# Where the low parts of the first MLP's weights and activations are subtracted, and how the decay products are formed

## The chip, the cores and the metric

The kernel runs on one core of one Trainium2 chip. The metric is the device time of one execution in microseconds. The core has five engines that each run their own queue in order: TensorE (PE in the profile; PEld is its weight load), VectorE (DVE), ScalarE (ACT), GpSimd (POOL), and SyncE (SP), which issues transfers. GpSimd issues transfers too.

## What is computed

Three parts follow each other: a linear attention with a decay per step, an MLP over all tokens, and a second stage with eight experts of which each token uses two.

```python
for t in range(S):                                   # 4 batches, 8 heads, S = 768, D = 48
    S_re, S_im = a[t] * (S_re + i S_im) + outer(k[t], v[t])     # a[t] complex, |a| <= 0.999
    y[t] = q[t] @ S_re
x = y.reshape(3072, 384)
h = x @ w_in                                         # 384 x 2048, w_in and w_out are float64
g = where(h > 0, h, exp(h) - 1)
x = g @ w_out                                        # 2048 x 384
logits = x @ w_gate + log1p(exp(x @ w_noise)) * noise
out[tok] = sum over the top two e of weight * relu(x @ w1[e]) @ w2[e]
```

## The kernel before

**Numbers.** TensorE runs its large products in the fast 32-bit format (fp32r), which keeps fewer bits than float32. Each factor is therefore split into a high part (the value rounded to fp32r) and a low part (the value less the high part), and a product is three products: high by high, high by low, low by high.

**Stages.** The attention is cut into 12 units (6 chunks of 128 steps by 2 pairs of batches). A unit has pieces `p` (magnitude and angle of the decay), `o`, `t` (sine, cosine, arctangent on ScalarE), `m` (decay products), `a`, `b` (scores, state, output `y`, its transpose `xt` with high and low part). The first MLP of unit u (`f`) follows in eight steps `s`: `l1(s)` makes 2 x 128 rows of `h` on TensorE (18 products, line 850), ScalarE and VectorE make `ge` out of it (lines 854 to 856), ScalarE its high part `gh` (line 859), VectorE its low part `gl` (line 860), and `l2(s)`, issued two steps later (`LAG = 2`), multiplies with the second weights (line 874). After every second unit, `route` picks the experts and eight indirect writes on GpSimd's queue (line 967) put the tokens into `table`. The eight experts follow.

**The first MLP's weights.** They come as float64 in 32 blocks of 128 x 384 (16 of `w_in`, 16 of `w_out`). For each block GpSimd issues the transfer (line 483), VectorE decodes the 64-bit values into `wf` with four instructions (lines 467 to 469 and 484), ScalarE rounds them to the high part (lines 507, 525), and TensorE forms the low part in PSUM: `ident` times `raw` in float32, then `minus` (the negative identity) times the high part is added to it (lines 509 and 510; 521 and 527 for `w_out`). ScalarE copies it out (lines 511, 528). For `w_out` the gate's weights are multiplied in as well: three transposes (line 517), a copy (519), three narrow products (523), a copy of the high part (526). The tiles of this stage use the same buffers as the MLP's: `raw` those of `xh` and `xl`, `wf` those of `gh` and `gl`, `woT` that of `ge`, `wtp` that of `ph`, `wlo` that of `y2`. So the MLP of unit 0 starts only behind the last block.

**The decay products.** `m_pieces` makes the running product over 128 steps with VectorE multiplications: seven over strides of 8 (`cm1`), four that double the reach (`cm2`) and one wide one (`cm3`), lines 633, 639 and 644, for each of the 12 units.

**Order.** `PAR` gives each piece a place in program order. Then `arrange` takes all instructions, gives each a cost by engine and shape, and lays them out by a list schedule (longest remaining path first); that order is each engine's queue. A tile of a ring of buffers may not start before the first users of the one before it (`roots`). `PAR['EARLY']` is 8, and there are 8 pairs of blocks, so that the branches `late` of `fetch`, `load_w_in` and `load_w_out` are never taken and place `x` is empty.

Of the kernel before, what the change touches and what calls it, by code (L numbers as in the profile page):

```python
# [27 lines left out]
def arrange(tc):  # L28
# [58 lines left out]
    def cost(n):  # L87
        i, k, c = ins[n], kinds[n], cells[n]
        if eng[n] == "PE":
# [25 lines left out]
        if eng[n] == "DVE":  # L115
# [16 lines left out]
        if k == "Memset":  # L132
            return 100 + c * .55, 100 + c * .55
        return 25, 25
# [5 lines left out]
    for n, i in enumerate(ins):  # L140
        e = eng[n]
        p = prev.get(e)
        if e == "PE" and p is not None and kinds[n] == kinds[p] == "Matmult":
            a, b = acc[p][0], acc[n][0]
            same = a[0] == b[0]
# [205 lines left out]
def tile_kernel(ctx, tc, q, k, v, a_re, a_im, w_in, w_out, w_gate, w_noise, noise, w1, w2, qp, kp, vp, ap,  # L351
# [42 lines left out]
    minus = consts.tile([128, 128], F32R, name="minus")  # L394
    ts(minus, jp, 0.0, -1.0, op0=OP.is_equal, op1=OP.mult)
# [62 lines left out]
    wbad = consts.tile([128, 2, 2 * FB], F32, name="wbad")  # L458
# [12 lines left out]
    def fetch(piece, f, n, late):  # L471

        tagf = "ge" if late else ("gh", "gl")[n % 2]
        t = wf.tile([128, Dm], F32, name="wf", tag=tagf, bufs=2)
        if not wide:
            nc.gpsimd.dma_start(*piece(f, 0, Dm, t))
            return t
        for z, (a, b) in enumerate(((0, 256), (256, Dm)) if late else ((0, Dm),)):
            if late:
                raw = wa.tile([128, 256, 2], I32, name="raw", tag="n4", bufs=4)[:, :b - a]  # L480
            else:
                raw = wf.tile([128, Dm, 2], I32, name="raw", tag=("xh", "xl")[n % 2], bufs=2)
            nc.gpsimd.dma_start(*piece(f, a, b, raw))
            nc.vector.tensor_reduce(wbad[:, z, n:n + 1], raw[:, :, 1].bitcast(F32), axis=AX.X, op=OP.min,
                                    apply_absolute_value=True)
            decode(raw, t[:, a:b])
        return t
# [15 lines left out]
    def load_w_in(f, late):  # L503
        raw = fetch(w_in_piece, f, f, late)
        WI[f] = [wts.tile([128, KD, 128], F32R, name=f"wi{x}", tag="wi") for x in "hl"]
# [7 lines left out]
    def load_w_out(f, late):  # L513
        raw = fetch(w_out_piece, f, FB + f, late)
# [9 lines left out]
        hi, lo = WO[f] = [wts.tile([128, WC], F32R, name=f"wo{x}", tag="wo") for x in "hl"]  # L524
# [1054 lines left out]
```

## Time and profile before

| | us |
|---|---|
| median of 3 executions | 1257.93 (1257.11 to 1259.96) |
| profiled execution, its own time | 1253.42 |
| span of that execution, first to last instruction | 1251.6 |
| busy in the span: TensorE | 1160.8 (93%) |
| VectorE | 786.7 (63%) |
| ScalarE | 648.9 (52%) |
| GpSimd | 234.4 (19%) |

The span is what the trace shows; 1.82 us of the execution lie outside of it. Busy shares over the whole span mix stages with different limits, so the rows below are by stretch: the weights are loaded from 0 to 131.5 us (beside the attention of the first units), attention and first MLP run from there to about 642 us, the last units' MLP to about 800 us, and the experts to the end.

### The profile page before, as it was taken

To read this page: it belongs to the slowest core of one execution; us is meant where nothing else is said; L and a number is where in the kernel's file an instruction comes from. 1 tells how busy PE (TensorE), PEld (TensorE's weight loads), DVE (VectorE), ACT (ScalarE), POOL (GpSimd) and SP (SyncE) were. 2 spreads that over 40 slices of the span, in tenths; PEclk is the share of its full clock that TensorE was granted. 3 is DMA by queue.
4 is the path that set the end of the run, shared out by engine and by line. 5 is a ranking of instruction groups with operands and counts; after the bars stand their busy time and mean duration, and the time that the engine had idled before them with its cause. 6 is when DMAs were issued, how large, how long until landed. Compare 5 with 4: busy or idle time off the path is not lost.

```text
span 1251.6 us, 22832 instructions
## 1 busy us (share of the span) xinstructions
PE 1160.8 (93%) x8821; PEld 1070.9 (86%) x8821; DVE 786.7 (63%) x1782; ACT 648.9 (52%) x1299; POOL 234.4 (19%) x265
## 2 busy tenths in 40 slices
PE   4786998999999999899999999799999999999997
PEld 2464988888998999899999898789898989898996
DVE  5798998987987979697863556344434343443322
ACT  6877876768776777576554464332323232332111
POOL 2111000002002000200200302432424242424222
PEclk9697999999999999899999999999999999999999
DMA  6345520220220202120100133343424242423111
GB/s 218 118 160 179 182 81 24 72 94 12 84 75 21 81 22 79 18 92 31 30 11 28 52 103 119 109 127 96 134 90 136 83 137 85 131 85 108 36 45 34
DMA packets 64309, 107.05 MB, mean 86 GB/s; under 512 B 19967, under 2 KB 46310, under 8 KB 64192
## 3 DMA queue, kind: packets, MB, share of 16 engines
q1 hardware_dynamic: 50096, 65.65, 16.9%
q0 software_dynamic: 14096, 39.86, 10.2%
q8 instruction: 71, 1.16, 0.4%
q14 instruction: 46, 0.38, 0.1%
HBM read 86.98 MB, written 20.70 MB: 86 GB/s over the span
## 4 chain that ended last, share of the span: by engine, by line
PE 51%; DVE 25%; issue 14%; ACT 6%; DMA 2%; POOL 2%; POOLq 0%; SPq 0%; DVEq 0%; ACTq 0%
PE mpo L1096 18%; PE mph L1074 17%; PE ph L850 4%; PE y L874 4%; DVE gl L860 2%; DVE ge L856 2%; DVE E L633 2%; DVE X L701 2%; PE mtp L1059 1%; DVE P L783 1%; DVE KK L692 1%; DVE Sc L770 1%; PE sc L779 1%; ACT L577 1%; POOL table L967 1%
## 5 line engine op out<-in xcount | busy, mean ns | idle before, releaser
L1076 ACT ACTIVATE egh<-mph 128x320 fp32r<-128x320 f32 (+1 forms) x128 | 66.3, 518 | 233.9 <-PE mpo L1096 141.7
L967 POOL DMA_INDIRECT table<-route x48 | 47.1, 981 | 593.4 <-DVE route L961 275.4
L1096 PE MATMUL mpo<-weh,egh 128*128 128x384 f32 (+1 forms) x448 | 151.6, 338 | 0.0
L1096 PE MATMUL mpo<-weh,egl 128*128 128x384 f32 (+1 forms) x448 | 151.6, 338 | 0.0
L1096 PE MATMUL mpo<-wel,egh 128*128 128x384 f32 (+1 forms) x448 | 151.2, 337 | 0.0
L874 PE MATMUL y<-woh,gh 128*128 128x400 f32 x384 | 138.9, 362 | 0.0
L1101 DVE SCALAR_TENSOR_TENSOR ac<-mpo,slots,ac 128x384 f32<-128x384 f32 (+1 forms) x49 | 30.2, 617 | 171.5 <-PE mpo L1096 171.5
L874 PE MATMUL y<-woh,gl 128*128 128x400 f32 x384 | 133.0, 346 | 3.1 <-DVE gl L860 3.1
L874 PE MATMUL y<-wol,gh 128*128 128x400 f32 x384 | 131.5, 342 | 0.0
L1077 DVE SCALAR_TENSOR_TENSOR egl<-mph,egh 128x320 fp32r<-128x320 f32 (+1 forms) x128 | 75.1, 587 | 80.2 <-ACT egh L1076 80.2
L850 PE MATMUL ph<-xh,wih 128*128 128x256 f32 x576 | 106.4, 294 | 8.1 <-DVE ge L856 8.1
L1027 ACT ACTIVATE weh<-raw 128x384 fp32r<-128x384 f32 x128 | 65.3, 522 | 84.2 <-PE mpo L1096 60.0
L850 PE MATMUL ph<-xl,wih 128*128 128x256 f32 x576 | 101.5, 285 | 0.0
L850 PE MATMUL ph<-xh,wil 128*128 128x256 f32 x576 | 101.4, 285 | 0.0
L1104 POOL DMA_INDIRECT out_dram<-ac,slots x56 | 55.2, 987 | 239.4 <-DVE ac L1101 216.4
L850 PEld LDWEIGHTS ph<-xh,wih 128*128 128x128 f32 x576 | 88.4, 193 | 12.0 <-DVE ge L856 7.5
L854 ACT ACTIVATE ge<-ph 128x512 f32<-128x512 f32 x96 | 57.2, 596 | 63.5 <-DVE gl L860 39.7
L859 ACT ACTIVATE gh<-ge 128x512 fp32r<-128x512 f32 x96 | 60.1, 628 | 54.8 <-PE y L874 51.8
L860 DVE TENSOR_TENSOR gl<-ge,gh 128x512 fp32r<-128x512 f32 x96 | 66.2, 690 | 34.9 <-ACT gh L859 34.2
L856 DVE SCALAR_TENSOR_TENSOR ge<-ge,ph 128x512 f32<-128x512 f32 x96 | 65.5, 683 | 33.6 <-ACT ge L855 32.3
L1028 DVE TENSOR_TENSOR wel<-raw,weh 128x384 fp32r<-128x384 f32 x128 | 69.3, 555 | 23.9 <-ACT weh L1027 22.1
L850 PEld LDWEIGHTS ph<-xh,wil 128*128 128x128 f32 x576 | 83.8, 193 | 0.0
(207 smaller groups left out, 2831.9 us busy)
## 6 DMA issues: line engine op xcount, KB each, us to landing
raw<-in_moe_w_dram SPq DMA_DIRECT2D x128, 192.0 KB, 2.6
nat_a<-in_a_rows_dram SPq DMA_DIRECT2D x24, 512.0 KB, 3.6
raw<-in_moe_w_in_dram POOLq DMA_DIRECT2D x16, 384.0 KB, 3.7
raw<-in_moe_w_out_dram POOLq DMA_DIRECT2D x16, 384.0 KB, 3.5
q<-in_q_pairs_dram SPq DMA_DIRECT2D x24, 256.0 KB, 3.7
k<-in_k_pairs_dram SPq DMA_DIRECT2D x24, 256.0 KB, 2.8
vt<-in_v_rows_dram SPq DMA_DIRECT2D x24, 192.0 KB, 2.7
out_dram<-zero SPq DMA_DIRECT2D x24, 192.0 KB, 4.5
```

Source lines behind the costliest of these rows:

```text
L850: mm(ph[:, j, :], w[:, z, :], x[:, z, :], start=n == 0, stop=n == 3 * KD - 1)
L856: stt(e, e, -1.0, ph, op0=OP.add, op1=OP.max)
L859: act(gh, e, AF.Copy)
L860: tt(gl, e, gh.bitcast(F32), op=OP.subtract)
L874: mm(d["y"][i], g[:, j, i * L:(i + 1) * L], w, start=s == 0 and j == 0 and n == 0, stop=s == NS - 1 and j == 1 and n == 2)
L967: st = nc.gpsimd.indirect_dma_start(out=table[:, :], out_offset=bass.IndirectOffsetOnAxis(ap=idx, axis=0), in_=row, in_offset=None)
L1027: act(w[0], raw, AF.Copy)
L1028: tt(w[1], raw, w[0].bitcast(F32), op=OP.subtract)
L1074: mm(ph[:, :n], w[:, z, :], x[:, z, :], start=k == 0, stop=k == 3 * KD - 1)
L1076: act(gs[0][:, f, :n], ph[:, :n], AF.Relu)
L1077: stt(gs[1][:, f, :n], ph[:, :n], 0.0, gs[0][:, f, :n].bitcast(F32), op0=OP.max, op1=OP.subtract)
L1096: mm(po[:m], x[:, f, o:o + m], w, start=k == 0, stop=k == 3 * FE - 1)
```

## The change

The low part of the weights is subtracted on GpSimd from `raw` and the high part in SBUF, so `minus`, the products with `ident` and `minus` and ScalarE's copies of the low part are gone. For `w_out` the 16 gate columns stay in PSUM and VectorE subtracts their low part. `gl` is subtracted on GpSimd too. The running product is eight scans (`tensor_tensor_scan`) of 128 steps for each unit in the place of twelve multiplications. The unused `late` branches go, and `wbad` has one plane. In `arrange`, GpSimd's subtraction and the scan get costs, products of 64 x 128 tiles get a cost and count as one run, and a ring's next tile waits for one first user of the one before it, not for all of them.

```diff
-PAR = {'EARLY': 8, 'x': (-0.25, 0.3), 'w': (0.15, 1.0), ...
+PAR = {'w': (0.15, 1.0), ...
...
+            if i.tile_size[1] == 128 and i.tile_size[0] == 64:
+                return 117, 330
...
+            if getattr(i, "is_tensor_tensor_scan", False):
+                return 58 + c * 2.084, 150 + c * 2.084
...
+        if k in ("TensorTensor", "TensorReduce"):
+            s = 160 + c * (2.1 if k == "TensorTensor" else 1.3)
+            return s, s + 40
...
-                roots = [x for x in p if not (deps[x] & mine)]
+                roots = [next(x for x in p if not (deps[x] & mine))]
...
-    minus = consts.tile([128, 128], F32R, name="minus")
-    ts(minus, jp, 0.0, -1.0, op0=OP.is_equal, op1=OP.mult)
...
+    def load_w_in(f):
+        WI[f] = [wts.tile([128, KD, 128], F32R, name=f"wi{x}", tag="wi") for x in "lh"][::-1]
         hi, lo = (w.rearrange("p c f -> p (c f)") for w in WI[f])
+        raw = fetch(w_in_piece, f, f)
         act(hi, raw, AF.Copy)
-        p = psf.tile([128, Dm], F32, name="wlo", tag="ph" if late else "y2", bufs=2)
-        mm(p, ident, raw, start=True, stop=False)
-        mm(p, minus, hi, start=False, stop=True)
-        act(lo, p, AF.Copy)
+        nc.gpsimd.tensor_tensor(lo, raw, hi.bitcast(F32), op=OP.subtract)
...
         act(wT, tp, AF.Copy)
-        p = psf.tile([128, WC], F32, name="wlo", tag="ph" if late else "y2", bufs=2)
-        mm(p[:, :Dm], ident, raw, start=True, stop=False, skip_group_check=True)
+        p = psf.tile([128, WC - Dm], F32, name="wlg", tag="y2", bufs=2)
         for c in range(KD):
-            mm(p[:, Dm:], wT[:, c, :], wg[:, c, :], start=False, stop=False, skip_group_check=True)
+            mm(p, wT[:, c, :], wg[:, c, :], start=c == 0, stop=c == KD - 1)
         act(hi[:, :Dm], raw, AF.Copy)
-        act(hi[:, Dm:], p[:, Dm:], AF.Copy)
-        mm(p, minus, hi, start=False, stop=True, skip_group_check=True)
-        act(lo, p, AF.Copy)
+        act(hi[:, Dm:], p, AF.Copy)
+        tt(lo[:, Dm:], p, hi[:, Dm:].bitcast(F32), op=OP.subtract)
+        nc.gpsimd.tensor_tensor(lo[:, :Dm], raw, hi[:, :Dm].bitcast(F32), op=OP.subtract)
...
+        def cum(q):
             def f():
+                x = ET[u][:, q]
+                nc.vector.tensor_tensor_scan(x, x, ones, 1.0, op0=OP.mult, op1=OP.mult)
             return f
...
+        for q in range(NP):
+            P.append((0.4, cum(q)))
+        P.append((0.1, least))
...
-                    tt(gl, e, gh.bitcast(F32), op=OP.subtract)
+                    nc.gpsimd.tensor_tensor(gl, e, gh.bitcast(F32), op=OP.subtract)
```

## Rows read from the trace of the kernel before

**Rows 1.** busy time by stretch: length, PE, PEld, DVE, ACT, POOL, clock, DMA share, GB/s
```profile
0.00:62.00 62.00, 35.26 (x114) 23.72 (x115) 40.74 (x106) 44.49 (x97) 13.77 (x32) 0.81 0.51 169
62.00:131.50 69.50, 54.46 (x372) 40.24 (x371) 64.11 (x142) 49.58 (x108) 8.38 (x15) 0.83 0.47 157
131.50:642.00 510.50, 479.44 (x4843) 457.49 (x4841) 439.91 (x1028) 359.09 (x688) 35.01 (x41) 0.99 0.19 61
642.00:800.00 158.00, 148.69 (x1027) 142.43 (x1025) 73.10 (x192) 71.46 (x143) 32.45 (x33) 1.00 0.25 73
800.00:1251.60 451.60, 442.99 (x2474) 407.00 (x2472) 168.82 (x317) 124.29 (x265) 144.75 (x145) 0.99 0.32 95
sum 1251.60, PE 1160.84 PEld 1070.88 DVE 786.68 ACT 648.90 POOL 234.36; mean PE 232.17 PEld 214.18 DVE 157.34 ACT 129.78 POOL 46.87
```

**Rows 2.** timeline of PE: last weight transposes, first product of the first MLP; start, us
```profile
128.38 0.55 PE L517 MATMUL wtp<-ident,wf 128*128 128x128 f32 x3
...
131.54 0.52 PE L850 MATMUL ph<-xh,wih 128*128 128x256 f32 x3
```

**Rows 3.** groups by line and shape, whole run: TensorE products that make the low part
```profile
L509 PE MATMUL wlo<-wf,ident 128*128 128x384 f32 x32 | 19.8, 712 | 20.7 <-DVE wf L469 19.2 <-ACT wol L528 1.2 <-ACT wil L511 0.2
...
L521 PE MATMUL wlo<-wf,ident 128*128 128x384 f32 x32 | 17.9, 651 | 0.0
...
L510 PE MATMUL wlo<-wih,minus 128*128 128x384 f32 x16 | 12.3, 771 | 0.1
...
L527 PE MATMUL wlo<-woh,minus 128*128 128x400 f32 x16 | 8.1, 505 | 1.6 <-ACT woh L526 1.5
```

**Rows 4.** the same view: ScalarE copies of the low part out of PSUM
```profile
L528 ACT ACTIVATE wol<-wlo 128x400 fp32r<-128x400 f32 x16 | 8.0, 502 | 4.4 <-PE wlo L527 4.4
...
L511 ACT ACTIVATE wil<-wlo 128x384 fp32r<-128x384 f32 x16 | 7.8, 487 | 4.1 <-PE wlo L510 3.8
```

**Rows 5.** who waited for whom, 0 to 131.5 us: total us, times, longest
```profile
DVE pa L551 <- ACT pb L550: 4.2, 4, 1.4
...
DVE pc L555 <- ACT pc L554: 4.1, 2, 2.7
...
DVE al L664 <- ACT X L578: 4.0, 2, 2.7
...
ACT wol L528 <- PE wlo L527: 4.2, 6, 1.4
...
ACT wil L511 <- PE wlo L510: 3.8, 5, 1.1
```

**Rows 6.** groups by line and shape: VectorE work replaced, and nearest rows for new work
```profile
L633 DVE TENSOR_TENSOR E<-E 128x128 f32<-128x128 f32 x84 | 34.3, 408 | 1.6 <-ACT E L625 1.1
...
L639 DVE TENSOR_TENSOR E<-E 128x64 f32<-128x64 f32 x48 | 13.5, 282 | 0.2
...
L644 DVE TENSOR_TENSOR E<-E 128x840 f32<-128x840 f32 x12 | 12.5, 1040 | 0.0
...
L860 DVE TENSOR_TENSOR gl<-ge,gh 128x512 fp32r<-128x512 f32 x96 | 66.2, 690 | 34.9 <-ACT gh L859 34.2
...
L664 DVE TENSOR_TENSOR al<-X,E 128x16 f32<-128x16 f32 x10 | 1.9, 194 | 4.0 <-ACT X L578 4.0
...
L1012 POOL MEMSET ac<- 128x384 f32 x5 | 2.0, 430 | 14.5 <-PE py L801 14.5
```

**Rows 7.** who waited for whom, TensorE's waits from 131.5 to 800 us
```profile
PE mtp L1059 <- DMA xr<-xs,slots: 9.1, 5, 4.4
...
PE ph L850 <- DVE ge L856: 8.1, 11, 2.1
...
PE tp L815 <- DVE X L607: 0.2, 1, 0.2
```

**Rows 8.** timeline of GpSimd, first and last table write of one routing
```profile
289.83 1.03 POOL L967 DMA_INDIRECT table<-route  x1 [179.08 <-DVE route L961]
...
299.55 0.96 POOL L967 DMA_INDIRECT table<-route  x1 [0.30 <-issue]
```

More of the change, by code (lines that the diff above doesn't have):

```diff
@@ L144, in arrange @@
             a, b = acc[p][0], acc[n][0]
-            same = a[0] == b[0]
+            same = a[0] == b[0] or tuple(i.tile_size) == tuple(ins[p].tile_size) == (64, 128) and not i.is_transpose
             r32 = "32r" in str(i.ins[0].dtype)
@@ L457, in tile_kernel @@
     wide = w_in.dtype != F32
-    wbad = consts.tile([128, 2, 2 * FB], F32, name="wbad")
+    wbad = consts.tile([128, 1, 2 * FB], F32, name="wbad")
     nc.vector.memset(wbad, 1.0)
@@ L469, in decode, with fetch @@
         stt(ti, low, 29, ti, op0=OP.logical_shift_right, op1=OP.bitwise_or)
-    def fetch(piece, f, n, late):
-        tagf = "ge" if late else ("gh", "gl")[n % 2]
-        t = wf.tile([128, Dm], F32, name="wf", tag=tagf, bufs=2)
+    def fetch(piece, f, n):
+        t = wf.tile([128, Dm], F32, name="wf", tag=("gh", "gl")[n % 2], bufs=2)
         if not wide:
@@ L477, in fetch @@
             return t
[L478 to L486, printed above, removed]
+        raw = wf.tile([128, Dm, 2], I32, name="raw", tag=("xh", "xl")[n % 2], bufs=2)
+        nc.gpsimd.dma_start(*piece(f, 0, Dm, raw))
+        nc.vector.tensor_reduce(wbad[:, 0, n:n + 1], raw[:, :, 1].bitcast(F32), axis=AX.X, op=OP.min,
+                                apply_absolute_value=True)
+        decode(raw, t)
         return t
@@ L501, in tile_kernel, with load_w_out @@
     wg = consts.tile([128, KD, 2 * E], F32, name="wg")
-    def load_w_in(f, late):
-        raw = fetch(w_in_piece, f, f, late)
-        WI[f] = [wts.tile([128, KD, 128], F32R, name=f"wi{x}", tag="wi") for x in "hl"]
+    def load_w_in(f):
+        WI[f] = [wts.tile([128, KD, 128], F32R, name=f"wi{x}", tag="wi") for x in "lh"][::-1]
         hi, lo = (w.rearrange("p c f -> p (c f)") for w in WI[f])
+        raw = fetch(w_in_piece, f, f)
         act(hi, raw, AF.Copy)
-        p = psf.tile([128, Dm], F32, name="wlo", tag="ph" if late else "y2", bufs=2)
-        mm(p, ident, raw, start=True, stop=False)
-        mm(p, minus, hi, start=False, stop=True)
-        act(lo, p, AF.Copy)
-    def load_w_out(f, late):
-        raw = fetch(w_out_piece, f, FB + f, late)
+        nc.gpsimd.tensor_tensor(lo, raw, hi.bitcast(F32), op=OP.subtract)
+    def load_w_out(f):
+        lo, hi = [wts.tile([128, WC], F32R, name=f"wo{x}", tag="wo") for x in "lh"]
+        WO[f] = hi, lo
+        raw = fetch(w_out_piece, f, FB + f)
         tp = psf.tile([128, KD, 128], F32, name="wtp", tag="ph", bufs=2)
@@ L628, in m_pieces, with least @@
             P.append((0.5, size(i)))
[L630 removed]
+        def cum(q):
             def f():
[L632 to L645 removed]
+                x = ET[u][:, q]
+                nc.vector.tensor_tensor_scan(x, x, ones, 1.0, op0=OP.mult, op1=OP.mult)
+            return f
+        def least():
             nc.vector.tensor_reduce(guard[:, u, :, 3], ET[u][:, :, L - 1].rearrange("p (i h) -> p i h", i=NB),
                                     axis=AX.X, op=OP.min)
[L648 to L654 removed]
+        for q in range(NP):
+            P.append((0.4, cum(q)))
+        P.append((0.1, least))
         return P
@@ L1121, in place @@
         t0, ln = PAR[cls]
-        if cls not in "wx":
+        if cls != "w":
             t0 += u + PAR.get((cls, u), 0.0)
@@ L1187, in tile_kernel @@
     NS = FB // 2
-    EARLY = PAR.get("EARLY", NS)
-    wp = {False: [], True: []}
+    wp = []
     for sx in range(NS):
-        late = sx >= EARLY
         for g in (load_w_in, load_w_out):
             for f in (2 * sx, 2 * sx + 1):
-                wp[late].append((1.0, lambda g=g, f=f, late=late: g(f, late)))
-    place("w", 0, wp[False])
-    place("x", 0, wp[True])
+                wp.append((1.0, lambda g=g, f=f: g(f)))
+    place("w", 0, wp)
     fk = [x for s in range(NS + LAG) for x in ([(1, s - LAG)] if s >= LAG else []) + ([(0, s)] if s < NS else [])]
@@ L1234, in tile_kernel @@
     place("t", NU, t_pieces(None, NU - 1))
-    rules += [(("w", 0), at("b", 0, "xt")), (at("a", 0, "qq", 1), ("x", 0)), (("x", 0), ("k", 1)), (("x", 0), ("q", 1)),
+    rules += [(("w", 0), at("b", 0, "xt")),
               (("z", 0), at("f", 0, "fin"))]
-    for sx in range(EARLY, NS):
-        for z in range(2):
-            n = 4 * (sx - EARLY) + 2 * z + 1
-            i = fk.index((z, sx))
-            rules.append((("x", 0, slice(n, n + 1)), ("f", 0, slice(i, i + 1))))
     settle(rules)
@@ L1286, in check @@
         if wide:
-            wo = wf.tile([128, 2, 2 * FB], F32, name="wok", tag="ge", bufs=2)
+            wo = wf.tile([128, 1, 2 * FB], F32, name="wok", tag="ge", bufs=2)
             ts(wo, wbad, SMALL, None, op0=OP.is_ge)
```

24 lines of the change are left out of this document (1 added, 23 removed).

## The prediction

> **What bounds the kernel now.** I read the busy time by stretch first, since the shares over the whole span mix stages with different limits. The last stretch, the experts, is TensorE at 443 of 452 us [rows 1]; the change doesn't touch it. From 131.5 to 800 us TensorE is busy 479.4 + 148.7 = 628.1 of 668.5 us (94%): 40.4 us of it idle. From 0 to 131.5 us no engine is full: TensorE 89.7, VectorE 104.9, ScalarE 94.1 us. Within it the second half is VectorE's (64.1 of 69.5 us, 92%) and the first is nobody's (40.7 of 62 us), which is the picture of a chain that passes between engines. The stretches meet where the timeline shows them to: the last weight transposes start at 128.38 us and the first product of the MLP at 131.54 us [rows 2], since the MLP uses the buffers of the weights. So the time is made of three terms: when the weights are done, how tightly TensorE is fed until 800 us, and a fixed rest. TensorE's work in the load stage counts only as far as it holds up the weights.
>
> **What the change takes away.** The low part costs TensorE 19.8 + 17.9 + 12.3 + 8.1 = 58.1 us of busy time [rows 3], nearly all ahead of 131.5 us, and ScalarE 8.0 + 7.8 = 15.8 us [rows 4]. None of these 58 us is time by itself: TensorE was idle for 131.5 - 89.7 = 41.8 us there. What it is worth must be read from what waited. VectorE was idle for 131.5 - 104.9 = 26.6 us, of which the three longest waits, 4.2 + 4.1 + 4.0 = 12.3 us, are for ScalarE, and ScalarE waited 4.2 + 3.8 = 8.0 us for just the products that go [rows 5]. With 15.8 us of copies and 8.0 us of waits gone from a ScalarE that was busy 94 of 131.5 us, most of VectorE's 12.3 us go too, and some waits further along. I take 10 us; the ends are 0 (VectorE is late anyhow in the second half) and 20 (three quarters of its idle time; the first transfer has to land in any case).
>
> The decay products: 34.3 + 13.5 + 12.5 = 60.3 us for 12 units, 5.0 us a unit [rows 6]. A scan is not in the trace. From below it costs half of a 128-element multiplication, 0.2 us; from above, two of them in a row, 0.82 us. The cost entry in the diff gives 58 + 128 x 2.084 = 325 ns, near the lower end and near the row of 408 ns; I take it. Eight make 2.6 us a unit, 31 us in all (13 to 79), so VectorE gains 29 us: 5 in the load stage (two units), 24 behind it (ten). The new subtraction of 16 gate columns is priced by the 128x16 row, 194 ns, 16 times: 3.1 us. VectorE in the load stage: 104.9 - 5 + 3 = 103 us, practically as before.
>
> `gl` leaves VectorE with 66.2 us [rows 6], all behind 131.5 us. VectorE's work from there to 800 us goes from 439.9 + 73.1 = 513 us [rows 1] to 513 - 66 - 24 = 423 us.
>
> **What it adds.** GpSimd gets 32 subtractions of 384 and 96 of 512 elements. No row shows one. From below: the memset of 384 elements, which reads nothing, 430 ns [rows 6]; from above, three times that for two reads and a write, 1.29 us, and by elements 1.72 us for 512. The diff's entry, 160 + 2.1 per element, gives 0.97 and 1.24 us, inside the ends, and I take it: 31 us in the load stage beside 22 us that GpSimd is busy there already, 119 us behind it beside 67. No bound by itself. [...]
>
> `gl` becomes 1.24 - 0.69 = 0.55 us longer. `l2` comes two steps behind `l1`, and a step is some 4 us of TensorE, so this is covered; if that cover were gone in each step it would cost 96 x 0.55 = 53 us. What is queued behind a waiting subtraction on GpSimd is the next transfer of weights (four `raw` buffers cover it), and in the MLP the table writes; what can stand ahead of it are the eight writes of a routing, from 289.83 to 300.5 us [rows 8].
>
> [...]
>
> What VectorE and GpSimd do to each other is the open cost. At least nothing; at most each subtraction holds up VectorE for its whole length, 31 us in the load stage. The nearest rows, memsets beside VectorE's work, show no harm, but a memset reads nothing. I take 4 us, since most of what is lost can fall into VectorE's idle time. The edits in `arrange` and the `late` branches I put at nothing: no branch `late` is taken, and the tile form that gets a cost is in none of the products that the rows name. But every queue is laid out anew, and that can go either way by several us.
>
> **The sum.** Load stage: -10 (ScalarE's waits) - 2 (VectorE's own work) + 4 = -8 us. From 131.5 to 800 us TensorE waited for VectorE eight times over by line, from 8.1 us down to 0.2 us, 20.1 us together, while the 9.1 us for gathered rows stay [rows 7]. With VectorE's load down by a sixth, I give back a quarter: -5 us. Together -13 us on the profiled execution's 1253.4 us, 1240.4 us. That execution was 4.5 us under the median (1257.93), so the forecast is 1245 us.
>
> **The rivals.**
> *GpSimd holds VectorE up (slower).* A first row speaks for weighing it: VectorE is at 92% in the second half of the load stage [rows 1], and the decode, two of whose four instructions read two tensors from SBUF, can't wait there. If three quarters of each subtraction are lost to VectorE, the load stage gets 0.75 x 31 = 23 us in the place of 4: -12 + 23 = +11 us. Behind it 0.6 x 119 = 71 us eat most of the 90 that VectorE gained, so those 5 us go too: 1253.4 + 11 + 4.5 = 1269 us. It decides from 12 us of lost VectorE time in the load stage on, 0.37 us for each subtraction. Against it: VectorE has 21 us idle in the first 62 us to swallow it. [...]
> *Nothing (same).* VectorE's 92% sets the end of the load stage whatever ScalarE and TensorE do, and the idle time behind it stays with the list schedule: -3 to +2 us, 1255 to 1260 us.
> *`gl` stands behind table writes (slower).* Of six routings, five fall among steps of the MLP; if each holds `gl` for the length of its writes, 10.7 us, and TensorE has half of it covered by `LAG`, it is 5 x 5 = 25 us against the 13 won: 1270 us. Against it: the writes have little behind them and `arrange` puts long paths first.
> *More than that (faster).* The load stage shrinks by the upper end of 20 us, and the 20 us of waits behind it go: 1253.4 - 40 + 4.5 = 1218 us.
> [...]
>
> **How the numbers follow.** The forecast (1232 to 1254 us) has 0.42, "nothing" 0.15, GpSimd against VectorE 0.24, table writes 0.09, more 0.10. Faster by over 0.2% (under 1255.4 us; 0.2% is about what a measurement of this kernel can tell) takes the forecast, "more" and a share of "nothing": 0.55. Same: 0.14. Slower: 0.31. The range of 1224 to 1272 us leaves out the far end of "more" and what is worse than the first rival. The forecast alone has 1232 to 1254 us.
>
> **What would show it.** Right: the first product of the MLP starts near 123 us and not at 131.5; VectorE's idle time ahead of it is under 20 us with few waits for ScalarE; TensorE's waits for VectorE from there on are near 15 us; a scan near 0.33 to 0.42 us; a GpSimd subtraction near 1.0 and 1.3 us. Lost to the first rival: decode instructions, 350 to 550 ns now, show longer durations or gaps where GpSimd subtracts, and the first product starts at 135 us or later. Lost to the table writes: `l2` waits for `gl` by several us at each routing. Wrong altogether if the first product moves by more than 20 us either way, or if TensorE's idle time between it and the experts changes by more than 15 us.

## The result

The changed kernel is slower: 1274.2 us (1272.88 to 1276.57) against 1257.5 us (medians of four executions each), a ratio of 1.0136 (95% interval 1.0120 to 1.0151). Its profiled execution took 1272.88 us (span 1270.9) against 1253.42 us (span 1251.6). The forecast was 1245 us, in a range up to 1272.

Three marks split the span: the first product of the MLP, the last product with the second weights (start of it), and the end. The first mark is not quite the end of the weights. In the kernel before, the first step of the MLP stands ahead of the last block's low part:

```profile
135.35 0.43 PE L527 MATMUL wlo<-woh,minus 128*128 128x400 f32 x1
```

It starts 3.8 us behind the MLP's first product of [rows 2], so unit 0 does not wait for the last block, though the description of the kernel says that it does. Where the weights end and the middle begins therefore depends on the mark by some us; the two stages together (+18.3 us) don't.

| | before, us | after, us | difference |
|---|---|---|---|
| load stage: 0 to the first product | 131.5 | 145.0 | +13.5 |
| middle: from there to the last product with the second weights | 625.4 | 630.2 | +4.8 |
| rest: experts | 494.7 | 495.7 | +1.0 |

Busy time by stretch of the changed kernel (length, PE, PEld, DVE, ACT, POOL, granted clock, DMA share, GB/s), to be laid beside [rows 1]:

```profile
0.00:62.00 62.00, 22.53 (x91) 19.17 (x92) 49.97 (x109) 42.92 (x85) 25.29 (x39) 1.00 0.50 163
62.00:145.00 83.00, 47.55 (x330) 40.97 (x329) 80.00 (x155) 43.46 (x94) 37.68 (x39) 0.59 0.43 142
145.00:655.00 510.00, 469.12 (x4786) 448.23 (x4784) 416.54 (x907) 352.59 (x679) 137.65 (x103) 1.00 0.20 60
655.00:800.00 145.00, 139.98 (x981) 134.22 (x980) 59.42 (x160) 69.95 (x142) 56.90 (x56) 1.00 0.23 66
...
sum 1270.90, PE 1136.32 PEld 1062.22 DVE 778.92 ACT 634.84 POOL 415.40; mean PE 227.26 PEld 212.44 DVE 155.78 ACT 126.97 POOL 83.08
```

TensorE has less to do, as meant (1136.3 us, 1160.8 before), and so has ScalarE. But VectorE, which was 40.7 + 64.1 us busy ahead of the first product, is now 50.0 + 80.0 us busy there, and 80.0 of 83 us (96%) in the second part. The timeline of PE shows the end of the load stage, against [rows 2]:

```profile
140.52 0.49 PE L516 MATMUL wtp<-ident,wf 128*128 128x128 f32 x3
...
141.73 0.74 PE L521 MATMUL wlg<-wg,woT 128*128 128x16 f32 x6
...
144.99 0.60 PE L832 MATMUL ph<-xh,wih 128*128 128x256 f32 x3
```

The groups by line and shape of VectorE in the load stage say what has grown (out<-in, count | busy, mean ns of one | idle before it). First the kernel before: the decode (467 to 469, 484) and one product of the attention:

```profile
L469 DVE SCALAR_TENSOR_TENSOR wf<-raw,wf 128x384 uint32<-128x384 uint32 x32 | 17.6, 550 | 0.2
L468 DVE SCALAR_TENSOR_TENSOR wf<-raw,wf 128x384 uint32<-128x384 uint32 x32 | 17.5, 547 | 0.0
L484 DVE TENSOR_REDUCE wbad<-raw 128x1 f32<-128x384 f32 x31 | 16.7, 543 | 0.0
L467 DVE TENSOR_SCALAR wf<-raw 128x384 uint32<-128x384 uint32 x32 | 11.2, 351 | 5.2 <-DMA raw<-in_moe_w_in_dram 3.7 <-ACT woh L525 1.4
...
L551 DVE TENSOR_TENSOR pa<-pa,pb 128x384 f32<-128x384 f32 x6 | 3.3, 554 | 4.2 <-ACT pb L550 4.2
```

and the same in the changed kernel, with the scans (628) and the subtraction of the gate columns (524):

```profile
L473 DVE SCALAR_TENSOR_TENSOR wf<-raw,wf 128x384 uint32<-128x384 uint32 x32 | 22.3, 697 | 0.0
L474 DVE SCALAR_TENSOR_TENSOR wf<-raw,wf 128x384 uint32<-128x384 uint32 x32 | 18.8, 586 | 0.1
L484 DVE TENSOR_REDUCE wbad<-raw 128x1 f32<-128x384 f32 x31 | 16.7, 539 | 0.0
L472 DVE TENSOR_SCALAR wf<-raw 128x384 uint32<-128x384 uint32 x32 | 14.6, 455 | 3.3 <-DMA raw<-in_moe_w_in_dram 3.3
L628 DVE TENSOR_TENSOR_SCAN E<-E,ones 128x128 f32<-128x128 f32 x16 | 10.4, 668 | 0.4 <-ACT E L620 0.4
L548 DVE TENSOR_TENSOR pa<-pa,pb 128x384 f32<-128x384 f32 x6 | 5.6, 928 | 2.4 <-ACT pb L547 2.4
...
L524 DVE TENSOR_TENSOR wol<-wlg,woh 128x16 fp32r<-128x16 f32 x16 | 2.6, 163 | 0.4 <-ACT woh L523 0.4
```

The two decode instructions with two tensors from SBUF (473, 474) went from 547 and 550 to 697 and 586 ns, the one with a single input (472) from 351 to 455, `pa` from 554 to 928. The reduction (484), one input as well, stayed at 539 to 543 ns: not everything on VectorE became slower. Over the stage the stretched instructions cost some 21 us (decode 4.8 + 1.2 + 3.4, scans 16 x 0.26 = 4.2 against the 408 ns that they take in e6, `pa` 2.3, and some 5 in smaller groups, each its busy time less that of as many at their old length).

GpSimd's subtractions, in the load stage and (842) in the whole run:

```profile
L525 POOL TENSOR_TENSOR wol<-wf,woh 128x384 fp32r<-128x384 f32 x16 | 24.0, 1500 | 16.6 <-ACT woh L522 16.4
L508 POOL TENSOR_TENSOR wil<-wf,wih 128x384 fp32r<-128x384 f32 x16 | 17.6, 1101 | 7.5 <-ACT wih L507 5.2 <-ACT woh L523 2.1
...
L842 POOL TENSOR_TENSOR gl<-ge,gh 128x512 fp32r<-128x512 f32 x96 | 135.3, 1411 | 421.0 <-ACT gh L841 366.5 <-ACT lg L867 22.3 <-DVE E L682 15.5
```

The shortest are 0.99 us for 384 and 1.26 us for 512 elements; the means are longer because some are held up in their turn (2.03 us for one of line 508 below). The timelines show who waits for whom. VectorE (start, us of one):

```profile
121.01 0.55 DVE L484 TENSOR_REDUCE wbad<-raw 128x1 f32<-128x384 f32 x1
121.47 1.43 DVE L474 SCALAR_TENSOR_TENSOR wf<-raw,wf 128x384 uint32<-128x384 uint32 x1
...
126.53 1.21 DVE L683 TENSOR_TENSOR X<-X,E 128x1024 f32<-128x1024 f32 x1
127.67 1.15 DVE L472 TENSOR_SCALAR wf<-raw 128x384 uint32<-128x384 uint32 x1
```

GpSimd in the same microseconds:

```profile
121.47 1.00 POOL L508 TENSOR_TENSOR wil<-wf,wih 128x384 fp32r<-128x384 f32 x1
...
126.57 2.03 POOL L508 TENSOR_TENSOR wil<-wf,wih 128x384 fp32r<-128x384 f32 x1 [1.11 <-ACT woh L523]
```

At 121.47 us both start; line 474, 0.55 us elsewhere, takes 1.43. At 126.57 it is GpSimd that comes second: behind VectorE's 1.21 us it takes 2.03 us in the place of 1.00, and then line 472 (0.35 us) stands behind it and takes 1.15. Each time the later one ends about when it would if it had begun at the other's end; an expectation below calls this the lock.

Waits of VectorE in the load stage, against [rows 5], and of TensorE in the middle (from 145 to 800 us), against [rows 7] (us in total, times, longest):

```profile
DVE wf L472 <- DMA raw<-in_moe_w_in_dram: 3.3, 1, 3.3
DVE pa L548 <- ACT pb L547: 2.4, 2, 1.4
```

```profile
PE sc L761 <- DVE sx L726: 9.1, 6, 2.0
PE ph L832 <- DVE ge L838: 8.2, 7, 1.6
PE sc L761 <- DVE X L665: 4.8, 5, 1.7
...
PE y L856 <- POOL gl L842: 0.6, 1, 0.6
```

VectorE's three long waits for ScalarE (12.3 us) are down to 2.8 us (2.4 of them for `pb`), as forecast. TensorE's waits for VectorE in the middle, though, rose over all lines from 26.4 to 34.0 us; the prediction's 20.1 us leave out 6.3 us for the routing.

### The profile page after: what moved, and what is told of

Its sections match the earlier page's. It is cut to its first block, busy times and chain, and to the rows that moved or that the text cites. A ratio compares the mean times of both kernels' runs of the same rounds, so it can differ in the third digit from the quotient of the medians.

```text
span 1270.9 us, 22689 instructions
## 1 busy us (share of the span) xinstructions
PE 1136.3 (89%) x8725; PEld 1062.2 (84%) x8725; DVE 778.9 (61%) x1653; ACT 634.8 (50%) x1267; POOL 415.4 (33%) x393
## 3 DMA queue, kind: packets, MB, share of 16 engines
q8 instruction: 70, 1.15, 0.4%
## 4 chain that ended last, share of the span: by engine, by line
PE 45%; issue 4%; DVE 3%; POOL 1%; DMA 1%; ACT 1%; POOLq 0%; DVEq 0%; ACTq 0%
PE mpo L1078 17%; PE mph L1056 16%; PE y L856 5%; PE ph L832 5%; PE mtp L1041 1%; POOL table L949 1%; DMA xr<-xs,slots 1%; PE sc L761 0%; DMA table<-route 0%; DVE ge L838 0%; POOL gl L842 0%; ACT ge L836 0%; PE py L780 0%; DVE E L628 0%; DVE KK L673 0%
## 5 line engine op out<-in xcount | busy, mean ns | idle before, releaser
L842 POOL TENSOR_TENSOR gl<-ge,gh 128x512 fp32r<-128x512 f32 x96 | 135.3, 1411 | 421.0 <-ACT gh L841 366.5
L856 PE MATMUL y<-wol,gh 128*128 128x400 f32 x384 | 131.5, 343 | 0.0
L1010 DVE TENSOR_TENSOR wel<-raw,weh 128x384 fp32r<-128x384 f32 x128 | 73.6, 591 | 33.0 <-ACT weh L1009 26.1
L1078 PEld LDWEIGHTS mpo<-wel,egh 128*128 128x128 f32 (+1 forms) x448 | 81.6, 182 | 2.9
L1078 PEld LDWEIGHTS mpo<-weh,egl 128*128 128x128 f32 (+1 forms) x448 | 81.4, 182 | 2.8
```

The source lines that it names most:

```text
L842: nc.gpsimd.tensor_tensor(gl, e, gh.bitcast(F32), op=OP.subtract)
L856: mm(d["y"][i], g[:, j, i * L:(i + 1) * L], w, start=s == 0 and j == 0 and n == 0, stop=s == NS - 1 and j == 1 and n == 2)
L1010: tt(w[1], raw, w[0].bitcast(F32), op=OP.subtract)
L1078: mm(po[:m], x[:, f, o:o + m], w, start=k == 0, stop=k == 3 * FE - 1)
```

## Experiments

**Theories.** *Reads*: GpSimd's subtraction and a VectorE instruction that takes two tensors from SBUF hold each other up, and this eats the gain. *Lateness*: GpSimd takes nearly twice VectorE's time (1.26 us at the shortest for a `gl`, where VectorE took 0.69 in the mean), so what it hands back or holds (`wf`, `ge`, `gl`) comes late. *Clock*: without the products TensorE runs its rest at a lower granted clock (0.59 from 62 us to the first product, where it had 0.83 before). *Layout*: the edits in `arrange` order the queues worse.

Each ratio is to executions of the kernel before taken beside the run; the marks are those of one profiled execution each. The last column is the start of the last instruction that writes a low part of the weights.

| run | ratio to before, 95% interval | first product | last product, second weights | middle | last low part |
|---|---|---|---|---|---|
| before | 1 | 131.5 | 756.9 | 625.4 | 135.8 |
| after | 1.0136 [1.0120, 1.0151] | 145.0 | 775.2 | 630.2 | 144.5 |
| e5: edits of the order alone | 1.0065 [1.0041, 1.0089] | 136.3 | 768.1 | 631.8 | 140.8 |
| e6: e5 + scans | 0.9929 [0.9907, 0.9951] | 128.4 | 749.7 | 621.3 | 128.4 |
| e7: e5 + `gl` on GpSimd | 1.0262 [1.0230, 1.0294] | 129.6 | 786.3 | 656.7 | 134.2 |
| e2: e5 + weights on GpSimd | 1.0133 [1.0110, 1.0156] | 139.4* | 774.3 | 634.9 | 152.7 |
| e9: scans + weights on GpSimd | 1.0084 [1.0052, 1.0117] | 144.3 | 772.0 | 627.7 | 146.2 |
| e1: scans + `gl` on GpSimd | 0.9994 [0.9976, 1.0012] | 132.6 | 759.4 | 626.8 | 131.6 |
| e8: after, weights on VectorE | 1.0122 [1.0093, 1.0152] | 125.0* | 770.8 | 645.8 | 137.5 |
| e4: after, products kept | 1.0103 [1.0082, 1.0123] | 141.7 | 768.4 | 626.7 | 140.4 |
| e3: after, weights' part by memsets | 1.0036 [1.0020, 1.0052] | 129.5 | 763.0 | 633.5 | 128.8 |
| e11: e7, `gl` by memsets | 0.9971 [0.9952, 0.9989] | 130.3 | 755.1 | 624.8 | 137.0 |
| e13: e11, late | 1.0141 [1.0124, 1.0158] | 131.5 | 777.1 | 645.6 | 136.1 |
| e14: e3, late | 1.0086 [1.0069, 1.0103] | 133.0 | 765.0 | 632.0 | 132.0 |
| e15: e13 and e14's edits on after | 0.9906 [0.9889, 0.9924] | 133.8 | 748.7 | 614.9 | 135.8 |
| e16: e1, `gl` late without reads | 0.9895 [0.9859, 0.9930] | 128.5 | 750.6 | 622.1 | 127.5 |
| e17: after, both late without reads | 0.9934 [0.9917, 0.9951] | 130.5 | 751.8 | 621.3 | 129.8 |
| e10: before + scans, old order rules | 0.9921 [0.9899, 0.9943] | 129.4 | 747.4 | 618.0 | 129.3 |
| e12: after, old ring rule | 1.0433 [1.0389, 1.0477] | 148.3 | 807.8 | 659.5 | 144.0 |

*In these two the first step of the MLP stands furthest ahead of the last low part, by some 13 us. In seven others, the kernel before among them, it stands 1.9 to 6.7 us ahead, so a few us between load stage and middle are a matter of the mark. The experts take 492 to 497 us in every run.

### Which part costs

**e1_w_undone.** The weights' low part goes back to TensorE:

```diff
-        nc.gpsimd.tensor_tensor(lo, raw, hi.bitcast(F32), op=OP.subtract)
+        p = psf.tile([128, Dm], F32, name="wlo", tag="y2", bufs=2)
+        mm(p, ident, raw, start=True, stop=False)
+        mm(p, minus, hi, start=False, stop=True)
+        act(lo, p, AF.Copy)
...
```

> Undoes one part: the low part of the weights is made on TensorE again (identity products, copies on ScalarE); scans, gl on GpSimd and the new list schedule stay. Theory (GpSimd's reading subtractions hold up VectorE while the weights are decoded): the decode instructions go back to 350 and 550 ns, the first product of the MLP starts at 126 to 132 us in the place of 145.0, and the time is 1253 to 1262 us. Rival 'order' (the new schedule with its loosened rings lays attention ahead of the weights): the first product stays at 140 us or later, 1268 us or more. Rival 'clock' (without the products TensorE's clock falls and the chain through its transposes gets longer): like the theory, since the products are back; it is told apart by the run that keeps them without use.

**e2_w_only.** The other way round: `gl` on VectorE (`tt(gl, e, gh.bitcast(F32), op=OP.subtract)`) and the multiplications back, the weights on GpSimd.

> One part alone: only the low part of the weights on GpSimd; gl on VectorE and the twelve multiplications as before, with the new schedule. Theory: VectorE is held up in the load stage as in the changed kernel, 15 to 25 us of longer instructions, first product at 138 to 148 us, 1265 to 1278 us. Rival 'other parts' (the loss comes from gl on GpSimd or the scans): 1250 to 1260 us.

**e5_schedule_only.** All three parts undone; what stays are the edits in `arrange` (costs, runs, ring rule) and of the `late` branches.

> The kernel before with the edits of the list schedule alone (loosened rings, new costs, the empty branches gone). Theory (the loss is the weights' low part on GpSimd): 0.997 to 1.003 of before, first product of the MLP at 129 to 134 us. Rival 'order' (the loosened rings cost part of it): 1.004 or more.

**e6_scan_only** is e5 with the scans, **e7_gl_only** is e5 with `gl` on GpSimd.

> Low parts of weights and activations as before, only the decay products as scans, with the new schedule. Without GpSimd beside it a scan took 408 ns, in steps of some 330, so VectorE saves 2.3 us a unit, 28 us in all. Theory: VectorE has slack behind the load stage, so 0.994 to 1.000 of before. Rival (VectorE is what TensorE waits for from 131.5 us on, as the prediction had it): 0.990 or less.

> Only the low part of the activations on GpSimd, with the new schedule. Theory: 96 readings of 1.3 us hold up VectorE there too, but VectorE loses 66 us of its own and is not what sets the pace: 0.996 to 1.004 of before; first product to first product of the second weights near 18 us (before: 11.6), since a step waits for the longer subtraction. Rival (the lock costs here as in the load stage): 1.006 or more.

**e9_gl_undone** is the changed kernel with `gl` on VectorE.

> The changed kernel with gl back on VectorE (weights' low part on GpSimd and scans as in it). If the loss lies only in the load stage (GpSimd's reads holding up the decode), first product of the MLP stays at 140 to 146 us, and the time stays within 4 us of the changed kernel: 1270 to 1276 us. If gl on GpSimd costs by itself in the MLP stage, as it did without scans (e7_gl_only, +23 us over e5_schedule_only), the time comes down to 1255 to 1266 us. If gl on GpSimd helps once the scans are in, it goes up to 1280 us or more.

Measured: with scans in, the weights on GpSimd cost 1.0136 / 0.9994 = 1.4% where `gl` is on GpSimd too, and 1.0084 / 0.9929 = 1.6% where it isn't; `gl` on GpSimd costs 0.9994 / 0.9929 = 0.7% and 1.0136 / 1.0084 = 0.5%. The scans are the part that gains: 0.9929 / 1.0065, 1.4%. In e1 the decode's two-input instructions are back at 546 and 548 ns and the first product at 132.6 us. Without the scans the parts don't add up: `gl` then costs 2.0% (e7 against e5) and the weights 0.7% (e2). e9, at 1267 us, and e6, at 0.9929, lie between their expectations; e5 and e7 came out as their rivals had it. e5 measures what the prediction put at nothing: the edits of the order alone cost 0.65%.

### Is it VectorE's time or GpSimd's?

**e8_w_on_vectore.** The 32 subtractions of the changed kernel by VectorE:

```diff
-        nc.gpsimd.tensor_tensor(lo, raw, hi.bitcast(F32), op=OP.subtract)
+        tt(lo, raw, hi.bitcast(F32), op=OP.subtract)
...
```

> The changed kernel with the weights' 32 subtractions on VectorE in the place of GpSimd. VectorE gets 32 x 0.46 = 15 us of work of its own and loses the 21 us for which it was held up. Theory: first product at 132 to 141 us, 1258 to 1270 us, a little better than the change. Rival 'GpSimd is merely slow' (a late low part, not VectorE, sets the end of the load stage): first product ahead of 130 us, under 1256 us.

Groups by line and shape of VectorE, the subtractions of e8:

```profile
L508 DVE TENSOR_TENSOR wil<-wf,wih 128x384 fp32r<-128x384 f32 x16 | 8.8, 550 | 0.2
L525 DVE TENSOR_TENSOR wol<-wf,woh 128x384 fp32r<-128x384 f32 x16 | 8.8, 550 | 0.9 <-ACT woh L522 0.8
```

VectorE spends 17.6 us on them, the decode is back at 350 and 548 ns, and the time is that of the changed kernel (1.0122 against 1.0136, intervals that overlap). The first product, at 125.0 us, came as early as the rival had it, but it stands ahead of the last blocks; the time is the theory's. Giving VectorE the whole work costs it no more than GpSimd's doing it beside it.

### The clock

**e4_products_kept.** The changed kernel with `ident` and `minus` products of the 16 `w_in` blocks issued again, their result unread.

```diff
+        p = psf.tile([128, Dm], F32, name="wlo", tag="y2", bufs=2)
+        mm(p, ident, raw, start=True, stop=False)
+        mm(p, minus, hi, start=False, stop=True)
```

> The changed kernel, and the two identity products of each of the 16 blocks of w_in are run on TensorE as well into a PSUM tile that nobody reads. Rival 'clock': TensorE's granted clock from 62 us to the first product goes from 0.59 to 0.8 or more and the time falls by 5 us or more. Theory: VectorE sets the pace, the time stays or grows: 1272 to 1280 us.

Busy time by stretch, second part of the load stage (columns as above):

```profile
62.00:141.70 79.70, 57.75 (x352) 43.23 (x351) 77.94 (x152) 42.56 (x93) 40.41 (x39) 0.64 0.48 151
```

The granted clock is 0.64 there, 0.59 in the changed kernel and 0.83 before; VectorE stays at 78 of 80 us, and the kernel is 0.3% faster (1.0103 / 1.0136, intervals that just overlap). The products brought the clock up only a little, so this run can't settle it. Four runs below can: e3, e14, e15 and e17 have a granted clock of 0.59 to 0.61 from 62 us to their first product, and that product at 129.5 to 133.8 us. The low clock stays in them and the loss of the load stage goes, so the clock is not its cause.

### Reads or lateness

**e3_lo_memset** writes the weights' low part with two memsets on GpSimd, **e11_gl_memset** `gl` with three, in the kernel of e7. The low parts are left out so.

```diff
-        nc.gpsimd.tensor_tensor(lo, raw, hi.bitcast(F32), op=OP.subtract)
+        for _ in range(2):
+            nc.gpsimd.memset(lo.bitcast(F32), 0.0)
...
```

> The changed kernel with two memsets of 384 elements on GpSimd (0.8 us, nothing read) in the place of each of the 32 subtractions, costed in the schedule like one subtraction; the low part of the weights is left out (zero) from the computation. Theory (what hurts is that GpSimd reads beside VectorE): VectorE's decode instructions are back at 350 and 550 ns and the first product starts at 118 to 130 us, 1246 to 1260 us. Rival 'queue' (what hurts is that GpSimd is busy and issues the transfers late) and rival 'clock': first product at 140 us or later, 1268 us or more.

> e7_gl_only (multiplications, weights' low part on TensorE, gl on GpSimd) with three memsets of gl in the place of each subtraction: the low part of the activations is left out (zero). GpSimd takes about as long (3 x 0.43 to 0.5 us against 1.4 us) and gl is ready as late, but nothing is read. If GpSimd's reads holding up VectorE cost the 23 us, it comes to 1245 to 1260 us. If the lateness of gl, or GpSimd's queue, or the layout of the queues costs them, it stays at 1275 to 1290 us.

Both win the loss back: e3 1.0036 with the first product at 129.5 us and the decode's two-input instructions at 545 and 546 ns; e11 0.9971 where e7 had 1.0262. But these memsets wait for no high part and hold no buffer, so they take away the lateness too. The next three put it back by short subtractions around the memsets: **e13_gl_late** in e11's kernel (the edit below), **e14_lo_late** for the weights' low part in the changed kernel, **e15_both_late** for both in the changed kernel.

```diff
-                    nc.gpsimd.tensor_tensor(gl, e, gh.bitcast(F32), op=OP.subtract)
+                    nc.gpsimd.tensor_tensor(gl[:, :, :4], e[:, :, :4], gh[:, :, :4].bitcast(F32), op=OP.subtract)
+                    for _ in range(2):
+                        nc.gpsimd.memset(gl[:, :, 8:].bitcast(F32), 0.0)
+                    nc.gpsimd.tensor_tensor(gl[:, :, 4:8], e[:, :, 4:8], gh[:, :, 4:8].bitcast(F32), op=OP.subtract)
```

> e11_gl_memset with the lateness put back: in the place of each subtraction of gl GpSimd subtracts 4 columns a half, writes the rest with two memsets, and subtracts 4 more columns; so it waits for gh, holds ge and delivers gl as late as a subtraction does, but hardly reads. The low part of most activations is left out (zero). If long reads against VectorE are what cost e7_gl_only its 1283 us, it comes to 1248 to 1262 us, with the product s of sx and al (two SBUF inputs) at 0.55 to 0.6 us and not 0.73. If the lateness of gl (and of ge, which it holds) does, it is 1272 us or more and ScalarE waits for GpSimd's gl by 20 us as in e7_gl_only.

> The changed kernel with the weights' low part written so: 4 columns subtracted, two memsets, 4 columns subtracted, 32 times; it waits for the high part and holds raw's decoded tile as long as a subtraction does. The low part of most weights is left out (zero). If the reads cost the load stage its time, it is e3_lo_memset again: first product of the MLP at 128 to 133 us, 1257 to 1264 us. If GpSimd's lateness in handing buffers back costs it, first product at 140 us or later, 1268 us or more.

> The changed kernel with both kinds of subtraction replaced so (weights and gl): all of the change's moves, queues and lateness, without long reads by GpSimd. The low parts of most weights and activations are left out (zero). If reads against VectorE are all that spoils the change, it shows what the change would have brought: 1240 to 1252 us, the forecast. If the moves bring nothing even so, 1253 to 1262 us. If it stays at 1266 us or more, the reads were not the cause.

e14 and e15 came out on the side of the reads, e13 on the side of lateness: 1.0141, with the product of `sx` and `al` at 547 ns and ScalarE waiting 49.5 us for GpSimd's `gl`. None of the three is clean: `arrange` had laid a memset ahead of the first short subtraction, or both behind the second, so that `ge`, `wf` and the results came free earlier than with a subtraction. With memsets over `gl[:, :, 2:]` and `lo[:, 2:]`, which overlap both short ones, the order holds: **e16_gl_held** does so for `gl` in e1's kernel, **e17_both_held** for both in the changed kernel.

> e1_w_undone (scans, gl on GpSimd, weights' low part on TensorE; ratio 0.9994) with each subtraction of gl replaced by 4 columns a half subtracted, two memsets over the rest, and 4 more columns subtracted, in this order (the memsets overlap both): gl is ready and ge is given back 1.3 us or more behind gh, as with a subtraction, but hardly anything is read. The low part of most activations is left out (zero). If the reads cost the MLP stage, it comes to a ratio of 0.980 to 0.992 (1230 to 1246 us), below e6_scan_only or level with it. If the lateness does, it stays at 0.996 or more.

> The changed kernel with both kinds of subtraction (weights and gl) replaced so, the order held: unlike in e14_lo_late and e15_both_late, wf, ge and the results come free as late as with a subtraction. The low parts of most weights and activations are left out (zero). If reads are the cause, it is level with e15_both_late: ratio 0.986 to 0.995, first product of the MLP at 131 to 136 us. If lateness is, it is above 1.005, first product at 139 us or later. Between these, both.

e17's timeline of GpSimd shows one `gl` made so, 0.44 + 1.10 + 0.23 us, no shorter than a subtraction (start, us of one):

```profile
434.73 0.44 POOL L852 TENSOR_TENSOR gl<-ge,gh 128x8 fp32r<-128x8 f32 x1 [11.70 <-ACT gh L851]
435.23 1.10 POOL L854 MEMSET gl<- 128x508 f32 x2
436.41 0.23 POOL L855 TENSOR_TENSOR gl<-ge,gh 128x8 fp32r<-128x8 f32 x1
```

It takes 0.9934 against the changed kernel's 1.0136, with the first product at 130.5 us. All moves and waits of the change are in it, with GpSimd busier than in the changed kernel (78 against 63 us of the load stage); the long reads are not. VectorE in its load stage (groups by line and shape):

```profile
L478 DVE SCALAR_TENSOR_TENSOR wf<-raw,wf 128x384 uint32<-128x384 uint32 x32 | 17.5, 547 | 0.1
L477 DVE SCALAR_TENSOR_TENSOR wf<-raw,wf 128x384 uint32<-128x384 uint32 x32 | 17.5, 546 | 0.0
L488 DVE TENSOR_REDUCE wbad<-raw 128x1 f32<-128x384 f32 x31 | 16.8, 541 | 0.0
L476 DVE TENSOR_SCALAR wf<-raw 128x384 uint32<-128x384 uint32 x32 | 12.5, 392 | 3.2 <-DMA raw<-in_moe_w_in_dram 3.2
L638 DVE TENSOR_TENSOR_SCAN E<-E,ones 128x128 f32<-128x128 f32 x16 | 6.4, 413 | 1.0 <-ACT E L630 1.0
```

Lines 477 and 478 are the decode with two inputs, at 546 and 547 ns again; the scan is at 413 where it was 668. For the middle, the state update from 150 to 770 us in the kernel before, the changed one (with `ge`, whose second input is in PSUM), and e16:

```profile
L770 DVE COPY Sc<-St 48x192 f32<-48x192 f32 x80 | 20.6, 258 | 1.3
...
L760 DVE TENSOR_TENSOR s<-sx,al 128x384 f32<-128x384 f32 x18 | 10.0, 558 | 0.1
```

```profile
L838 DVE SCALAR_TENSOR_TENSOR ge<-ge,ph 128x512 f32<-128x512 f32 x96 | 65.0, 680 | 74.9 <-ACT ge L837 68.1 <-issue 3.3 <-PE y L856 2.7
L752 DVE COPY Sc<-St 48x192 f32<-48x192 f32 x80 | 33.1, 413 | 0.9
...
L742 DVE TENSOR_TENSOR s<-sx,al 128x384 f32<-128x384 f32 x18 | 15.2, 846 | 0.0
```

```profile
L759 DVE COPY Sc<-St 48x192 f32<-48x192 f32 x76 | 23.9, 314 | 0.9
...
L749 DVE TENSOR_TENSOR s<-sx,al 128x384 f32<-128x384 f32 x17 | 9.3, 548 | 0.1
```

`s`, two inputs in SBUF, is 558, 846 and 548 ns. `ge`, one from PSUM, is 680 ns (683 before) beside the same subtractions. The copy of the state stays at 314 ns in e16, and line 476 in e17 at 392 ns (351 before): these one-input instructions are longer beside memsets, too. So the copy was in e11, where GpSimd makes `gl` by memsets alone: 339 ns, with `s` at 553. The rows shown say no more than this: `s` took 846 ns beside subtractions and 548 to 553 beside memsets, the copy 413 and 314 to 339 against 258, and the reduction 539 to 543 throughout. Why the forms of instruction differ so, no run shows.

So the reads cost 1.0136 / 0.9934 = 2.0%: 14.5 us in the load stage and 8.9 us in the middle, by the marks of after and e17. By the last low part it is 14.7 us and 8.7 us, so this split doesn't hang on the mark. `arrange` lays each of these runs out anew, and layout alone moved e5 by 0.65%, so the sizes carry some of that. The direction doesn't: the run with fewer long reads is the faster one in each of the seven pairs (after against e3, e14, e15 and e17, e1 against e16, e7 against e11 and e13), by 0.5 to 2.9%. What stays open: without the scans (e7, e13, e11) the middle is 656.7, 645.6 and 624.8 us, so lateness seems to cost there, too; with the scans e16 and e17 show none. Nor does ScalarE wait longer for `gl` in the changed kernel, before it may fill the next `ge`: 24.2 us for GpSimd's, where it waited 39.7 us for VectorE's before (131 to 800 us).

### The order

**e10_scan_old_rings** is the kernel before with the scans and their cost entry alone. **e12_after_old_rings** is the changed kernel with the old ring rule:

```diff
-                roots = [next(x for x in p if not (deps[x] & mine))]
+                roots = [x for x in p if not (deps[x] & mine)]
```

> The kernel before with the scans and their cost entry alone: low parts where they were, and the ring rule and the other costs in arrange as before. If the scans give 14 us by themselves and the edits in arrange cost 7 us (e5_schedule_only), it is the best so far: 1235 to 1241 us beside a kernel before at 1252 to 1257. If the edits in arrange are nothing once the scans are in, it is e6_scan_only again: ratio 0.990 to 0.995, some 1245 us. If the gain was a lucky layout of the queues, it is 1250 to 1260 us.

> The changed kernel with the old ring rule: a ring's next tile waits for all first users of the tile before it. If the loosened rule costs some 7 us wherever it is (e5_schedule_only), it is 1264 to 1270 us. If it is nothing here, 1272 to 1276 us. If the changed kernel needs it, because GpSimd's subtraction is one more user of raw and wf, it is slower than 1278 us.

The old rule costs the changed kernel another 2.9% (1.0433 / 1.0136), the contrary of what e5 made me expect, and with scans alone the old rules, ring rule and costs together, make no difference (e10 0.9921, e6 0.9929). ScalarE's waits for GpSimd's `gl` in the middle, after and then e12 (us, times, longest):

```profile
ACT ge L836 <- POOL gl L842: 24.2, 16, 3.3
```

```profile
ACT ge L836 <- POOL gl L842: 76.5, 52, 3.5
```

With the old rule the next `ge` stands behind GpSimd far more often. Why e5 lost 0.65% isn't settled; the same edits are worth nothing to e6.

e10's scans, whole run (groups by line and shape):

```profile
L633 DVE TENSOR_TENSOR_SCAN E<-E,ones 128x128 f32<-128x128 f32 x96 | 36.0, 407 | 0.2 <-ACT E L625 0.2
```

e6 and e10 are the kernels here that compute all and beat both: 0.7% and 0.8% under the kernel before.

## Why the prediction was wrong

**The step that failed first** is "I take 4 us" for what VectorE and GpSimd do to each other, with the memsets of [rows 6] as the nearest rows. It measured 14.5 us in the load stage (after against e17), and 8.9 us in the middle, for which the sum had no term at all. The memset was the wrong neighbour for just the reason that the prediction named and passed over: it reads nothing. Its ends, 0 and 31 us, held the value of the load stage. And "show no harm" was a misreading even of the memsets. A copy beside one of those in [rows 6], 0.42 us long elsewhere, took 0.73 us (timelines of VectorE, then GpSimd, kernel before; start, us of one):

```profile
642.01 0.73 DVE L683 COPY X<-X 64x512 f32<-64x512 f32 x1
...
642.05 0.42 POOL L1012 MEMSET ac<- 128x384 f32 x1 [14.46 <-PE py L801]
```

**The reason given for the small value** was that VectorE's idle time would swallow it. That held for a third of it. Of the 21 us, worked out as above for each part, some 7 lie in the first 62 us, where VectorE had 21 us idle and went from 40.7 to 50.0 us; some 14 lie in the second part, which had nothing to swallow them with (92% busy before, 96% after) and which sets the end. The idle time should have been read by part, as [rows 1] shows it.

**ScalarE's waits (-10 us)**: they went, and VectorE's idle time ahead of the first product fell from 26.6 to 15.0 us, and to 19.0 us in e17. The load stage hardly gained even there by the first product: 130.5 us, -1.0. By the last low part it gained 6.0 us (129.8 against 135.8). VectorE's work, forecast at -2, is 111.5 us in e17 against 104.9: 2.7 us for the gate columns, 1.3 us for line 476, 3.1 us less for scans in the place of multiplications, and some 6 us of pieces of the units that now lie ahead of the first product. What the 58 us that TensorE lost bought shows best over both stages: e17 ends them at 751.8 us, e16, which keeps that work on TensorE, at 750.6, so nothing. That is the rival *Nothing*; its reason, that VectorE's share sets the end, fits (94% busy in e17's second part) and isn't shown by a run of its own.

**The middle (-5 us)** is -4.1 us in e17 from the first product on, but +0.9 us from the last low part on, so its size can't be called right. What there was came from the scans: e6, with `gl` on VectorE, has the same 621.3 us. The 66 us of `gl` taken from VectorE bought nothing, and the reads turned -4.1 into +4.8 us. Altogether e17, without the reads, gains 0.66%, some 8 us, where the sum without its 4 us has 17; the scans alone gain as much (e6, e10). So the moves to GpSimd were overpriced as well.

**Right:** the scans gain. Their price was 0.325 us; measured 36.0 / 96 = 0.375 us of busy time (407 ns each; only where several stand in a row do they come closer: five at 389.58 us of the changed kernel take 1.67 us, 0.33 each) where GpSimd doesn't read, so 24 us saved and not 29, and 20 in the changed kernel. GpSimd's 0.97 and 1.24 us measured 0.99 and 1.26 at the shortest. `LAG` covers `gl`: TensorE waits 0.6 us for it in all, which also ends the rival of the table writes. The clock fell to 0.59 in the second part of the load stage; the sum has no term for it, and rightly: e17 has 0.60 there and its first product at 130.5 us.

**The first rival** had the cause, the place and nearly the price: +11 us in the load stage and the 5 us behind it lost, 1269 us. Measured were +13.5 and, where it has 0, +4.8, so 1274 us and not 1269. It was given 0.24. What spoke for it, a decode at 92% with two SBUF inputs, was on the page; what spoke against it, idle time in another part of the stage, should not have outweighed that.

**The edits of the order**, at nothing and "either way by several us", cost 0.65% alone (e5), while one of them, the ring rule, saves the changed kernel 2.8% (1.0136 / 1.0433).

**Two readings in the sum** were off without moving it much: 96 scans at the lower end of 0.2 us make 19 us and not 13, and TensorE waited for VectorE 26.4 us and not 20.1, of which a quarter is 6.6 and not 5 us.

## What to carry to other kernels

Before work goes to GpSimd, list VectorE's instructions in the stretch where it will run: those with two tensors in SBUF, and one-input copies and scalar operations, were longer beside GpSimd's subtractions here (547 to 697, 258 to 413 and 351 to 455 ns in the mean). In the load stage VectorE lost two thirds of GpSimd's 32 us so, and most of that came out as time, because VectorE was 92% busy in the part that sets the end. Ask of work taken from an engine whether that engine sets the end of the stretch: neither the 58 us of TensorE nor the 66 us of `gl` bought any time here. To tell contention from lateness, replace the operation by one as long, behind the same waits and with the same buffers held, that doesn't read, and make sure that the scheduler keeps its order.

## What had not been expected of the hardware

Beside memsets on GpSimd, which only write, VectorE's one-input instructions were longer: line 472's form went from 351 to 444 ns in e3, the state copy from 258 to 314 ns in e16 and to 339 in e11, while the two-input ones stayed at 545 to 553 ns. A subtraction of 4 columns a half (8 elements) on GpSimd took 0.19 us in e15, at 401.55 us, where 512 elements took 1.26 us at the shortest: some seventh of the time for a sixty-fourth of the elements. And moving 32 subtractions of 550 ns from VectorE to GpSimd (17.6 us) cost VectorE at least as much in waiting, some 21 us in the load stage, as in work.
